# One core, one list of 865 steps: the order of a fused sequence-mixing kernel drawn up anew

## The chip, the cores and the metric

The kernel runs on one core of a Trainium2 chip. The metric is device time in microseconds of one execution; lower is better. TensorE (PE), VectorE (DVE), ScalarE (ACT), GpSimd (POOL) and the DMA queues of SyncE (SP) and ACT work side by side. Each engine takes its own instructions strictly in the order of the program and waits at an instruction until what that one needs is there.

## The reference

Two branches over the same input of 2048 rows and 512 columns, mixed by a gate per row. Branch `a` is a diagonal linear recurrence with complex states, branch `b` is linear attention with 32 heads of width 16 and softmax feature maps.

```
g = sigmoid((x * gate_w).sum(-1))
# a: Lam_bar = exp(exp(log_dt) * Lam);  Bu = x @ B_bar.T
#    h[t] = Lam_bar * h[t-1] + Bu[t];   a = 2 * (h @ Cmat.T).real + x * Dskip
# b: q, k, v = x @ wqkv;  pq = q @ w_phi;  pk = k @ w_phi    (per head)
#    phi = concat(softmax(p), softmax(-p));  kv = phi_k.T @ v;  z = phi_k.sum(rows)
#    b = (phi_q @ kv / (phi_q @ z + 1e-6)) @ wo
out = g * a + (1 - g) * b
```

## The kernel before

The rows are cut into 16 tiles of 128; tile `ti` holds rows of one residue modulo 8, so that the recurrence is carried eight rows at a time. The kernel is written as small generators, `st_k`, `st_g` and so on, each of which makes one tile's worth of a stage and stops (`yield`) after each piece. A string, `ORDER`, says in which order the pieces are taken: each entry names a generator (letters and number), and taking the entry runs it to its next stop. `@` gives the PSUM banks that the piece takes, `:D` moves the evacuation of PSUM from ACT to DVE, `:A` sends an output through ACT's DMA queue instead of SP's, and `F:n` puts n idle matmuls.

The engines PE, DVE, ACT and SP are under a manual schedule: the list is their program order. There is no other scheduler for them, so an entry that is moved in the list moves on each engine and queue that it uses.

The entries:

- `NI`, `NR`: loads of the imaginary and the real part of B, 512 KB each (L287). `l8` to `l15`: transposing loads of row tiles 8 to 15 of x (L232); tiles 0 to 7 are loaded ahead of the list. `R`: transposes of B (L291). `Q`: transposing loads of the q weights (L295). `C`: transposing loads of C (L299). `J`: copies of the loaded C into two arrangements X1 and X2, two copies of 256 KB each (L304); `J0` and `J1` need C0, C2, C4 and C6, `J2` and `J3` need C1, C3, C5 and C7. `O`: load of wo. All of these are issued by SP.
- `W`, `f`, `w`: weights transposed and folded with w_phi. `V`, `U`, `P` to `P4`, `i`, `M`, `D`: parameters of the recurrence; `P2`, `P3` and `i` take sines and cosines on ACT. `L` loads the activation table set with Exp and Ln again, behind the sines.
- `k`, `v`, `q`: projections of a tile and their evacuation. `x`, `n`: maximum, minimum and differences for the softmaxes on DVE; `e`, `E`: the exponentials on ACT; `s`, `S`: sums, Ln, Exp and the multiply. `x0` to `x4` and so on are the key groups; `xA`, `nA`, `eA`, `sA` and those with capital letters (`X1` to `S3`) are the four query groups of four tiles. Step 8 of `sA` and of `S1` to `S3` is the multiply of L567; steps 9 to 12 send the four tiles through transposes into `phT` (L579), by SP, but for the last two tiles of the run, which PE transposes (L574).
- `a`: sums over the rows of key features times values; `Y` takes them out as `KVm`.
- `g`: Bu of residue r and state block j, `z` the scan over the blocks of eight rows, `h` the states of each residue. `c`: scaling of X1 and X2 (two multiplies on ACT, L603, and a sum).
- `y`, `o`, `t`: the outputs of a tile. `y`: h times C (L734) and the skip term (L739). `o`: query features times KVm (L753), division by way of Ln and Exp, and the transposing of the result, by SP (L775) or for the last four tiles by PE (L770). `t`: the product with wo (L782), the scaling by the gate (L786 on ACT, L788 on DVE) and the output DMA (L790).

How an entry is read:

```
    for tok in ORDER.split():
        tok, _, eng = tok.partition(":")
        tok, _, banks = tok.partition("@")
        sel["eng"] = "dve" if eng == "D" else "act"
        sel["q"] = nc.scalar if eng == "A" else nc.sync
        ...
        next(st[tok])
```

Exponentials and logarithms go through `aexp`, sines through `asin`; both note for the program's builder that they come behind the table load that they belong to (L132).

Of the kernel before, what the change touches and what calls it, by code (L numbers as in the profile page):

```python
# [864 lines left out]
```

## Time and profile before

| | |
|---|---|
| time, median of 3 runs | 157.53 us |
| lowest, highest | 156.07, 159.17 us |
| span of the profiled execution, first to last instruction | 153.7 us |
| median less span | 3.8 us |
| PE busy | 145.5 us (95%) |
| DVE busy | 131.0 us (85%) |
| ACT busy | 136.7 us (89%) |
| POOL busy | 12.9 us (8%) |
| granted TensorE clock, mean | 0.995 |

The profile is of one execution; its own time outside the program is not shown, so its span stands for it, and the difference to the median, 3.8 us, is what lies around it. Sums below are made on the span. Busy time counts an instruction from its start to its end as recorded; instructions of one engine overlap at their ends, and the ends of matmuls are modelled, so an engine with 99% busy time may still have small gaps. A releaser is who ended an engine's wait.

### The profile page before, as it was taken

Reading aid. Unit: us, or ns where it says so; the run is one execution under the profiler, and the core shown is the slowest. Engines: PE = TensorE matmul, PEld = TensorE weight load, DVE = VectorE, ACT = ScalarE, POOL = GpSimd, SP = SyncE. Lnnn points to the kernel's source line nnn. Section 1 sums busy time; section 2 is a strip of 40 time slices with the busy share of each in tenths; the row PEclk is TensorE's granted clock in tenths of the full one; section 3 lists DMA queues with packets and bytes.
Section 4 is the critical chain, followed back from the end, with each engine's and each line's share of the span. In section 5 each row is a group of like instructions: output and inputs, shape, how many; then the busy total and the mean of one; then the engine's idle time right before and its main releaser. Section 6 shows DMA issues by size and latency. Waiting matters only on the chain.

```text
span 153.7 us, 3412 instructions
## 1 busy us (share of the span) xinstructions
PE 145.5 (95%) x1238; PEld 99.7 (65%) x1254; DVE 131.0 (85%) x302; ACT 136.7 (89%) x322; POOL 12.9 (8%) x43
## 2 busy tenths in 40 slices
PE   7799999999999999999999999999999899999990
PEld 7656665886899858889876565554545455555550
DVE  3599999999999999999999999999999858445510
ACT  3599999999999999999999999999798897577672
POOL 8258800000000000000000000000000000000000
PEclk9999999999999999999999999999999999999998
DMA  4788995544474379960000006603139938667633
GB/s 117 162 220 121 213 171 102 102 86 92 101 102 100 80 146 205 237 133 0 2 4 2 0 0 134 125 18 68 33 82 118 215 80 194 141 118 172 211 123 102
DMA packets 48737, 17.03 MB, mean 111 GB/s; under 512 B 42064, under 2 KB 48720, under 8 KB 48720
## 3 DMA queue, kind: packets, MB, share of 16 engines
q1 hardware_dynamic: 47008, 15.36, 50.6%
q10 hardware_dynamic: 1552, 1.44, 2.9%
q8 instruction: 10, 0.16, 0.5%
q0 software_dynamic: 160, 0.01, 0.2%
q14 instruction: 7, 0.06, 0.1%
HBM read 2.64 MB, written 2.10 MB: 31 GB/s over the span
## 4 chain that ended last, share of the span: by engine, by line
ACT 48%; PE 31%; DMA 8%; DVE 6%; issue 3%; POOL 2%; ACTq 0%; POOLq 0%
PE py L734 12%; ACT EEk L140 12%; ACT uv L121 9%; PE py L782 6%; ACT vx L121 5%; PE pq L478 5%; ACT Xq L121 5%; ACT phT L603 4%; PE ph L685 3%; ACT va L121 3%; DMA phT<-EEq 3%; DMA oT<-on 3%; PE pn L753 2%; DMA vec_n<-in_A_log_dt_dram 2%; ACT EEq L140 2%
## 5 line engine op out<-in xcount | busy, mean ns | idle before, releaser
L614 PE MATMUL pgq<-xT,BT 128*128 128x256 bf16 x256 | 31.5, 272 | 0.0
L614 PEld LDWEIGHTS <-BT 128*128 128x128 bf16 x256 | 24.7, 98 | 3.5
L140 ACT ACTIVATE EEk<-EEk 128x1024 bf16<-128x1024 bf16 x20 | 21.3, 1099 | 0.0
L478 PEld LDWEIGHTS <-xT 128*128 128x128 bf16 x128 | 12.2, 97 | 11.0 <-issue 0.2
L121 ACT CAST uv<-pgq 128x512 bf16<-128x512 f32 x28 | 16.7, 638 | 0.0
L492 PE MATMUL pv<-Wv,xT 128*128 128x256 bf16 (+1 forms) x128 | 16.5, 273 | 0.1
L478 PE MATMUL pq<-Wq,xT 128*128 128x512 bf16 x60 | 15.2, 379 | 0.2
L782 PE MATMUL py<-Wo,oT 128*128 128x512 bf16 x59 | 14.7, 379 | 0.6 <-DMA oT<-on 0.3
L478 PE MATMUL pk<-Wk,xT 128*128 128x512 bf16 x60 | 14.9, 379 | 0.2
L492 PEld LDWEIGHTS <-xT 128*128 128x128 bf16 x128 | 12.5, 98 | 3.1 <-issue 0.2
L786 ACT ACTIVATE ot<-py,G 128x512 bf16<-128x512 f32 x15 | 9.8, 684 | 2.9 <-PE py L782 2.4
L140 ACT ACTIVATE EEq<-EEq 128x1024 bf16<-128x1024 bf16 x12 | 11.8, 1084 | 0.3 <-DVE EEq L535 0.3
L603 ACT ACTIVATE phT<-X,dgB 128x512 bf16<-128x512 bf16 x16 | 11.1, 751 | 0.0
L140 ACT ACTIVATE ld<-pn 128x16 f32<-128x16 f32 x32 | 6.4, 204 | 5.2 <-PE pn L753 5.0
L121 ACT CAST vx<-pv 128x256 bf16<-128x256 f32 x32 | 10.7, 435 | 0.0
L121 ACT CAST nu<-pn 128x256 bf16<-128x256 f32 x26 | 10.0, 400 | 0.0
L556 DVE TENSOR_TENSOR EEk<-EEk,rck 128x4096 bf16<-128x4096 bf16 (+1 forms) x5 | 9.3, 1860 | 0.1
L121 ACT CAST Xq<-pq 128x512 bf16<-128x512 f32 x16 | 9.0, 604 | 0.4 <-PE pn L753 0.4
L782 PEld LDWEIGHTS <-oT 128*128 128x128 bf16 x64 | 5.7, 98 | 5.7 <-DMA oT<-on 0.5
L753 PEld LDWEIGHTS <-phT 128*128 128x128 bf16 x128 | 6.4, 97 | 4.6 <-DMA phT<-EEq 1.3
L761 DVE TENSOR_TENSOR on<-nu,rd 128x512 bf16<-128x512 bf16 x16 | 6.6, 422 | 2.6 <-ACT rd L140 2.1
L519 DVE TENSOR_TENSOR smk<-smk 128x512 bf16<-128x512 bf16 (+4 forms) x18 | 8.1, 449 | 0.1
(179 smaller groups left out, 322.9 us busy)
## 6 DMA issues: line engine op xcount, KB each, us to landing
X<-HM SPq DMA_DIRECT2D x8, 256.0 KB, 4.7
out_dram<-ot SPq DMA_DIRECT2D x9, 128.0 KB, 2.2
out_dram<-ot ACTq DMA_DIRECT2D x7, 128.0 KB, 2.0
C2r<-in_B_wqkv_dram ACTq DMA_DIRECT2D x2, 256.0 KB, 3.5
Wv<-in_B_wqkv_dram SPq DMA_DIRECT2D x1, 512.0 KB, 4.0
Bn<-in_A_B_im_dram SPq DMA_DIRECT2D x1, 512.0 KB, 5.5
Bn<-in_A_B_re_dram SPq DMA_DIRECT2D x1, 512.0 KB, 5.9
Wo<-in_B_wo_dram SPq DMA_DIRECT2D x1, 512.0 KB, 5.9
```

The source lines that it names most:

```text
L121: nc.scalar.copy(out=out_ap, in_=in_ap)
L140: ins = nc.scalar.activation(**kw)
L478: MM(out=pt[:], lhsT=xT[:, kt, ti * P:(ti + 1) * P], rhs=W[:, kt, :], start=(kt == 0), stop=(kt == KT - 1))
L492: MM(out=pv[c][:], lhsT=xT[:, kt, ti * P:(ti + 1) * P], rhs=Wvg[:, kt, c * hd:(c + 1) * hd + c], start=(kt == 0), stop=(kt == KT - 1))
L519: VT(out=dst, in0=cur[:, :, :, 0:n, :], in1=cur[:, :, :, n:2 * n, :], op=op)
L556: VT(out=E5, in0=E5, in1=rc.to_broadcast([P, L, 2 * NB, Dh, 4]), op=ALU.mult)
L603: nc.scalar.mul(out=t_, in_=x_, mul=c_)
L614: MM(out=pg[:, h, :], lhsT=BT[:, kt, 2 * j + h, :], rhs=xT[:, kt, r * NC:(r + 1) * NC], start=(h == 0 and kt == 0), stop=(r % 2 == 0 and k ...
L734: MM(out=py[:], lhsT=hs(r, t, slice(a * P, (a + 1) * P)), rhs=C2B[t], start=(t == 0), stop=False)
L753: MM(out=pn[:, 4 * m:4 * m + 4, :].rearrange("p h e -> p (h e)"), lhsT=ph[:, 4 * hf + m, :], rhs=KVm[:, 4 * hf + m, :], start=(m == 0), st ...
L782: MM(out=py[:], lhsT=oT[:, g, :], rhs=Wo[:, g, :], start=False, stop=(g == HG - 1))
L786: nc.scalar.mul(out=ot[:], in_=py[:], mul=G[:, ti:ti + 1])
```

## The change

The string `ORDER` is replaced. It holds the same 865 entries. Their order is another, many PSUM banks are, and 30 entries have another engine or output queue: the evacuations of W2 and f1 go from ACT to DVE, the other 28 belong to the tail (o7 to o15, S3, t3 to t15). In both lists every Exp and Ln that comes after the sines stands behind `L`. Nothing else in the kernel is changed. Lines that neither the text nor the prediction speaks of are left out here.

```diff
--- before.py
+++ after.py
@@ -22,34 +22,34 @@
 ORDER = """
-NI l8 l10 F:28 W1@0 W0@1 W0 B W2@2 W2 NR W1:D W3@3 f1@4 f1 W3:D V@5 V U f0@6 U P P P2 U P2 P2 P2 P2 f0 f2@0 P4 P4 P4
-V2@1 V2 f2 l9 P3 i3 f3@3 f3 F:4 k1@2 k0@4 P P2 P3 l12 i1 i0 k0 gw i0 i3 U k1 i3 i3:D i3 i0 i1 i1 k2@5 k2 k3@6 k3 v0@03
-k4@1 i0:D x0 i1:D l11 x0 i1 n0 F:4 x0 k4 n0 R0 i2 n0 i0 x0 n0 k5@4 i2 i2 x0 i2:D n0 x1 x1 k5 n1 i2 v3@25 v0 x1 k7@6 k7
-k6@7 R1 L e0 n1 n1 x1 n1 l13 k6:D v4@14 x1 l14 v1@03 v1 k10@6 n1 x2 v4 n2 n2 n2 x2 e0 s0 x2 v3 v7@70 v7 l15 k8@3 v2@14
-v6@25 s0 s0 k9@7 k12@0 x2 Q1 e1 s0 v2 v6 s0 k11@1 s0 e1 M k11 k8 D k10 k9 R3 k12 g40@4 g40 s0 s1 g00@2 g00 n2 a0@51 a0
-v5@36 v5 s1 R5 x2 v8@70 R2 v8 C5 s1 s1 s1 s1 g60@4 n2 x3 s1 g60 g30@2 x3 n3 x3 n3 g10@3 C3 g20@6 e2 e2 e2 e2 x3 a1 a1
...
-a2 s3 C6 g21 g62 C2 C1 g11 g11 C0 J0 w0@6 w1@0 J2 J2 a2 g22@4 J0 w2@2 x4 s3 J1 g31 w1 w0 w3@7 g22 g31 z0 z0 z0 s3 w2
-s3 n4 z0 z0 w3 g61@0 g51@6 g51 g61 g02@4 g51 e4 g02 g71@3 g71 g71 g71 q3@2 s3 g12@7 g12 e4 q2@0 z0 g12 z1 q3 q1@6 q1
-q0@4 q2 z1 z0 h50@3 z1 z1 g42@7 q0 z1 z1 v10@26 h50 xA z1 h10@0 e4 e4 z1 g42 nA s4 g32@4 v10 g32 a3 g52@3 g32 h60@7 c2
-xA s4 c4 O g52 xA c4 R6 z1 z1 v9@26 s4 h10 g52 nA g72@4 g72 c4 h60 v9 a3 J3 g03@3 v11@26 c2 c2 s4 g72 g72 c0 c0 nA
...
-g73 g73 v13@26 v13 q10@0 z3 c6 z3 c5 sA z3 z3 v15@73 z3 a4 a4 a4 v15 z3 q10 q5@4 a4 Y z3 h31@0 q5 sA h30@4 z3 q9@2 h31
-q13@6 h31 q9 h33@0 h61@7 Y q13 h30 sA sA c5 h62@3 z3 z3 h30 h61 sA Y Y h22@5 q4@2 h62 q4 h33 q15@6 q11@7 h22 h20@4 h20
-h32@2 h32 sA sA c1 q11 h13@1 h13 h32 q14@3 h40@5 h33 c3 h53@7 h42@4 sA h42 h53 c1 c1 sA h21@2 c3 h21 q6@0 q6 q15 c6
-q7@1 h63@4 h63 q8@7 h03@0 c3 q7 c6 h40 sA c7 h41@6 h41 y6@2 c7 h03 h03 h43@4 h43 y2@1 h02@5 c7 sA h23@6 h23 h01@0
...
-o3 G S1 N2 S1 t2 o3 S1 o3 t2 t2:A q12@3 q12 N2 S1 S1 o1@4 o1 o1 o1 o1 S1 S1 E2 S1 y0 y4@1 y9@3 y8@4 y8 y8 X3 E2 E2 S1
-S1 S1 N3 X3 E2 t3 X3 X3 X3 S2 N3 t0 t0 t0:A S2 t3 S2 y1 t1 t1 y5 y9 y9 o4@7 o4 o4@0 o4 y4 o4 o4 o4 o5@5 o5 o5@7 o5 o5
-y13@0 S2 S2 o6@5 o6 o6@7 o6 o6 y13 N3 y7@5 y7 N3 y7 y13 o5 S2 S2 N3 E3 o5 o6 o6 S2 S2 E3 E3 o7@7 o7:D y4 t4 t4:D t5
-o7@7 S2 S2 E3 S3 t5 S2 S3 S3 o7 o7 o7 t6 y11@1 y11 o7 t6 o8@6 o8 o8@7 o8 o8 S3 S3 o8 y12@2 o9@6 o9 o9@7 o8 y11 y12 y12
-y10@6 o9 o9 o9 o11@7 o11 o9 S3 S3 y10 y10 o11@7 t7 o11 o11 t7 t8 S3 S3 o11 o11 S3 t8 S3@7 S3:D S3@5 S3 t9 t9 t1:A
-o10@4 y15@7 o10:D o10@5 o10:D t8 o10 o10 o10 y15 o12@4 o12:D o12@3 t4 o14@5 o12 o12 o12 t5 o14 t11 o14@4 o14:D o14 o14
-t11 y14@3 t9:A o13@5 o13 o12@4 o12:D y14 o13@1 o13 o13 o15@4 o15:D o15@5 o15 o15 t12 t3:A t10 o13 o13@1 o15 t6:A t11
-o14@4 o13:D t7 t10 t10 y15 t12 t12 o15@5 o15 y14 o14:D t13 t14 t14 t14 t13 t13 t15 t15 t15:A
+NI B l8 NR F:28 W0@2 W0 W1@1 W1:D W3@5 W3:D W2@6 W2:D l10 f1@0 f1:D f3@4 V@1 V U f3 P P P2 f2@6 P2 P2 P2 f0@0 f0 P P2
+P4 P3 f2 P2 P4 V2@5 F:4 k1@3 k1 U l12 P4 V2 P3 i3 k0@4 i1 i0 gw l9 i0 k0 i3 i3 k2@1 k2 i1 i3:D i3 n0 i0 i0:D x0 n0 i1
+l11 x0 k3@6 R0 R1 n0 x0 k3 v0@03 v0 U n0 x0 R3 i1:D i2 k4@2 F:4 k4 x0 i0 i2 v1@75 n0 k5@4 i1 x1 n1 v1 k5 k6@3 i2 i2:D
+i2 L x1 k7@6 k7 l15 v3@25 e0 e0 v4@41 v4 R2 n1 x1 n1 x1 U k6:D v3 n1 x1 l13 n1 M k8@0 x2 Q1 n2 l14 x2 v7@63 v7 s0 C2
+e1 k10@7 k8 v2@41 n2 v6@25 s0 x2 s0 n2 s0 s0 v6 v2 D k12@6 s0 s0 e1 s1 g00@3 g40@2 n2 k10 k12 k11@0 k11 k9@4 s1 k9
...
+g70 g70 z0 C7 w0@6 w0 a2 a2 g62 s3 a2 z0 s3 g21 a2 g22@3 g22 g61@6 g31 J0 w1@0 z0 z0 z0 z0 C1 J1 x4 g41 g61 g31 z0 z0
+n4 w3@7 g51@3 w3 w1 s3 g51 g51 s3 g02@2 g02 w2@4 z0 w2 g71@6 g71 q1@7 s3 q0@4 z0 g12@0 C5 e4 g12 g71 g71 z1 e4 h10@3
+z1 g12 h50@6 q1 e4 h10 q3@2 q2@0 g42@7 z1 z1 h50 h60@3 z1 q0 z1 h60 q3 J3 a3 q2 xA nA z1 z1 g32@6 e4 g32 v10@02 J2 J2
+J0 g42 g32 c2 g52@3 g52 nA v10 v9@07 c2 g52 s4 xA nA c2 g72@4 s4 v9 xA c4 c4 z1 z1 s4 g72 c4 xA v12@03 v11@72 s4 g03@6
...
+g53 eA q5@0 g73@7 g73 g73 g73 sA z3 z3 v13@34 sA z3 z3 sA q10@6 v13 q10 v15@27 v15 a4 a4 a4 h22@4 q5 c3 c3 h22 a4 Y
+h62@7 h31@0 h62 sA q9@2 c0 z3 Y z3 c3 q9 h32@2 q4@3 q13@4 z3 z3 sA h31 h31 sA Y G h20@7 h32 h32 q4 q13 h20 Y c1 q8@5
+c1 q15@0 h42@4 h30@7 q7@6 q7 h42 q11@3 q15 O q11 h33@3 z3 z3 c1 h41@1 h30 q14@6 h41 h13@4 h13 h53@2 c6 sA h53 q6@0 h30
+h33 h21@1 c7 sA h33 c6 h21 h23@4 y2@7 q8 c7 h43@3 h23 c6 y6@2 h63@5 c7 sA sA q6 h40@1 sA h40 y6 y2 h02@4 q14 h02 y0@1
...
+t2 G o3@3 S1 o3 o3 t2 N2 S1 o3 S1 N2 S1 o0 t0 t0 N2 o1@4 o1 o1 S1 o3 q12@7 q12 S1 S1 y8@3 E2 y4@1 y4 o1 y9@4 t3 S1 o1
+S1 E2 E2 E2 y9 X3 t1 N3 y8 X3 N3 X3 N3 y4 S1 X3 t3 S1 t1 o4@7 o4 S1 N3 o4@0 y5 X3 S2 o4 o4 y8 y9 S2 o5@5 o5 o5@7 o5 o5
+y13@0 o4 o6@5 o6 o6@7 o6 S2 S2 o6 o5 y13 y13 S2 o4 o5 N3 y7@5 S2 S2 o6 o7@7 o7 y7 y7 o6 E3 E3 E3 o7@7 S2 t4 S2 E3 S2
+S2 o7:D t4:D t5 t5:D t6 t6:D y11@1 S2 y11 o8@7 o7 t6:A S3 o8:D o8@6 o7 o7 o8 y12@2 o8 S3 o9@7 o9 o8 o9@6 o9 o9 S3 y11
+S3 S3 S3 y12 y10@6 o9 S3 o11@7 y10 y10 o11 o11@7 o11 o8 o9 S3 o11 o11 t7 t7:D S3 o11 t2:A y12 t0:A S3 S3@7 S3 t8 t7
+S3@5 S3:D t5:A y15@7 t8 t9 t9:D o10@5 o10 o10@3 o10:D o10 y15 y15 o12@5 o10 o12:D o12@3 o12 t3 t11 t11:D o14@3 o12 o14
+o14@4 o14 o14 y14@5 o13@3 o15@4 o13 o12 o10 o13@1 o13 o15:D y14 o12@3 o15@4 o13 t1:A t10 o14 o13 o13@1 o12 o14@3 o15:D
+o15 o15 t10:D t12 o13 t13 o15@6 t9 t4:A t11:A o15:D o14 y14 t14 t12:D t12 t10:A t14 t13:D t13:A t14 t15 t15:D t15:A t8
 """
```

More of the change, by code (lines that the diff above doesn't have):

```diff
@@ L30 @@
-v5@36 v5 s1 R5 x2 v8@70 R2 v8 C5 s1 s1 s1 s1 g60@4 n2 x3 s1 g60 g30@2 x3 n3 x3 n3 g10@3 C3 g20@6 e2 e2 e2 e2 x3 a1 a1
-n3 Q2 k15@7 g10 g10 k15 x3 n3 g20 k14@0 k14 s2 n3 R4 s2 k13@4 g01@3 Q0 k13 n4 s2 g30 g01 x4 s2 x4 Q3 n4 x4 g50@7 g70@6
-g30 g50 n4 x4 e3 e3 g41@0 g50 n4 R7 s2 g21@4 s2 g70 s2 C7 e3 g31@3 e3 s3 g62@2 C4 g70 g70 z0 g11@7 a2 z0 s3 g41 z0 a2
-a2 s3 C6 g21 g62 C2 C1 g11 g11 C0 J0 w0@6 w1@0 J2 J2 a2 g22@4 J0 w2@2 x4 s3 J1 g31 w1 w0 w3@7 g22 g31 z0 z0 z0 s3 w2
-s3 n4 z0 z0 w3 g61@0 g51@6 g51 g61 g02@4 g51 e4 g02 g71@3 g71 g71 g71 q3@2 s3 g12@7 g12 e4 q2@0 z0 g12 z1 q3 q1@6 q1
@@ L35 @@
-q0@4 q2 z1 z0 h50@3 z1 z1 g42@7 q0 z1 z1 v10@26 h50 xA z1 h10@0 e4 e4 z1 g42 nA s4 g32@4 v10 g32 a3 g52@3 g32 h60@7 c2
-xA s4 c4 O g52 xA c4 R6 z1 z1 v9@26 s4 h10 g52 nA g72@4 g72 c4 h60 v9 a3 J3 g03@3 v11@26 c2 c2 s4 g72 g72 c0 c0 nA
-g63@0 z2 z2 v12@74 a3 nA v11 a3 xA g03 z2 z2 z2 z2 xA nA s4 J3 g63 g23@2 c5 s4 v12 g23 h51@6 g13@3 g13 g13 z2 z2 c0 z2
-z2 eA g43@0 g43 eA v14@74 v14 J1 h51 s4 g33@2 g33 h52@3 g33 h12@0 g53@6 eA g53 g53 h12 h11@7 h11 h52 eA sA g73@4 g73
-g73 g73 v13@26 v13 q10@0 z3 c6 z3 c5 sA z3 z3 v15@73 z3 a4 a4 a4 v15 z3 q10 q5@4 a4 Y z3 h31@0 q5 sA h30@4 z3 q9@2 h31
@@ L40 @@
-q13@6 h31 q9 h33@0 h61@7 Y q13 h30 sA sA c5 h62@3 z3 z3 h30 h61 sA Y Y h22@5 q4@2 h62 q4 h33 q15@6 q11@7 h22 h20@4 h20
-h32@2 h32 sA sA c1 q11 h13@1 h13 h32 q14@3 h40@5 h33 c3 h53@7 h42@4 sA h42 h53 c1 c1 sA h21@2 c3 h21 q6@0 q6 q15 c6
-q7@1 h63@4 h63 q8@7 h03@0 c3 q7 c6 h40 sA c7 h41@6 h41 y6@2 c7 h03 h03 h43@4 h43 y2@1 h02@5 c7 sA h23@6 h23 h01@0
-h00@4 END q8 G X1 y6 y6 q14 y2 N1 X1 h00 h00 N1 y2 h02 h02 X1 N1 G h01 o0@6 y0@7 o0 o0@3 h01 o2@4 o2 X1 o2@5 o2 o2 N1
-y5@6 o0 y3@0 X1 N1 y5 X2 o0 o1@4 E1 o2 y0 o2 o0 E1 E1 E1 X2 y1@5 y1 y3 y3 o1 G N2 X2 N2 X2 o0 N2 X2 o3@3 o3 o3@4 S1 o3
@@ new lines @@
+l11 x0 k3@6 R0 R1 n0 x0 k3 v0@03 v0 U n0 x0 R3 i1:D i2 k4@2 F:4 k4 x0 i0 i2 v1@75 n0 k5@4 i1 x1 n1 v1 k5 k6@3 i2 i2:D
+i2 L x1 k7@6 k7 l15 v3@25 e0 e0 v4@41 v4 R2 n1 x1 n1 x1 U k6:D v3 n1 x1 l13 n1 M k8@0 x2 Q1 n2 l14 x2 v7@63 v7 s0 C2
+e1 k10@7 k8 v2@41 n2 v6@25 s0 x2 s0 n2 s0 s0 v6 v2 D k12@6 s0 s0 e1 s1 g00@3 g40@2 n2 k10 k12 k11@0 k11 k9@4 s1 k9
+a0@51 g40 x2 a0 v5@67 v5 s1 x2 g00 R6 s1 Q3 R5 s1 n2 v8@04 v8 s1 x3 g20@2 s1 e2 e2 n3 e2 g10@7 k13@3 g10 x3 g10 n3 e2
+x3 n3 x3 C0 Q2 g01@6 g20 a1 a1 k15@0 k14@4 k15 R4 C4 g60@7 g30@2 Q0 n3 g01 x3 s2 g60 C3 g30 n3 s2 k13 k14 n4 g30 s2 n4
@@ new lines @@
+s2 x4 n4 x4 n4 e3 e3 C6 s2 s2 g11@6 x4 s2 g50@7 g50 g50 R7 e3 e3 g31@4 g11 g11 g70@3 s3 x4 g21@0 g70 g41@2 s3 g62@7
+g70 g70 z0 C7 w0@6 w0 a2 a2 g62 s3 a2 z0 s3 g21 a2 g22@3 g22 g61@6 g31 J0 w1@0 z0 z0 z0 z0 C1 J1 x4 g41 g61 g31 z0 z0
+n4 w3@7 g51@3 w3 w1 s3 g51 g51 s3 g02@2 g02 w2@4 z0 w2 g71@6 g71 q1@7 s3 q0@4 z0 g12@0 C5 e4 g12 g71 g71 z1 e4 h10@3
+z1 g12 h50@6 q1 e4 h10 q3@2 q2@0 g42@7 z1 z1 h50 h60@3 z1 q0 z1 h60 q3 J3 a3 q2 xA nA z1 z1 g32@6 e4 g32 v10@02 J2 J2
+J0 g42 g32 c2 g52@3 g52 nA v10 v9@07 c2 g52 s4 xA nA c2 g72@4 s4 v9 xA c4 c4 z1 z1 s4 g72 c4 xA v12@03 v11@72 s4 g03@6
@@ new lines @@
+g72 g72 z2 a3 a3 v11 s4 v12 z2 g03 c0 nA z2 h11@4 a3 g43@2 c5 z2 J1 c0 J3 g43 h11 xA nA g63@0 g63 g23@3 z2 z2 h51@6 s4
+g13@7 h51 z2 z2 g13 c5 c5 z2 v14@20 g33@4 g23 g13 g33 z2 v14 h61@7 eA g53@6 h61 h12@3 h12 g33 g53 h52@2 h52 s4 eA eA
+g53 eA q5@0 g73@7 g73 g73 g73 sA z3 z3 v13@34 sA z3 z3 sA q10@6 v13 q10 v15@27 v15 a4 a4 a4 h22@4 q5 c3 c3 h22 a4 Y
+h62@7 h31@0 h62 sA q9@2 c0 z3 Y z3 c3 q9 h32@2 q4@3 q13@4 z3 z3 sA h31 h31 sA Y G h20@7 h32 h32 q4 q13 h20 Y c1 q8@5
+c1 q15@0 h42@4 h30@7 q7@6 q7 h42 q11@3 q15 O q11 h33@3 z3 z3 c1 h41@1 h30 q14@6 h41 h13@4 h13 h53@2 c6 sA h53 q6@0 h30
@@ new lines @@
+h33 h21@1 c7 sA h33 c6 h21 h23@4 y2@7 q8 c7 h43@3 h23 c6 y6@2 h63@5 c7 sA sA q6 h40@1 sA h40 y6 y2 h02@4 q14 h02 y0@1
+h00@0 h00 h01@6 sA h02 h63 h03@5 h00 h43 END X1 o0@3 o0 N1 X1 h01 N1 h01 y0 y0 o0@0 o0 G X1 o2@4 o2 N1 h03 X1 y2 N1
+h03 X1 N1 X2 o2@6 o2 o2 o2 y6 y3@0 o0 G o2 E1 E1 E1 E1 X2 y3 y3 N2 y1@5 y1 y1 X2 y5@6 y5 o0 X2 N2 o1@3 o3@4 o1 o3 X2
+t2 G o3@3 S1 o3 o3 t2 N2 S1 o3 S1 N2 S1 o0 t0 t0 N2 o1@4 o1 o1 S1 o3 q12@7 q12 S1 S1 y8@3 E2 y4@1 y4 o1 y9@4 t3 S1 o1
+S1 E2 E2 E2 y9 X3 t1 N3 y8 X3 N3 X3 N3 y4 S1 X3 t3 S1 t1 o4@7 o4 S1 N3 o4@0 y5 X3 S2 o4 o4 y8 y9 S2 o5@5 o5 o5@7 o5 o5
```

## The prediction

> **What bounds the kernel now.** I read the page first, then busy time by stretches, then the waits, the chain that ended last and the order of the SP queue. Stretches: start:end, length, then busy us of PE, weight loads, DVE, ACT, POOL, granted clock, DMA share, GB/s.
>
> ```profile
> span 153.7 us, 3412 instructions
> 0.00:10.00 10.00, 7.81 (x73) 6.42 (x75) 5.66 (x37) 5.64 (x10) 4.92 (x17) 1.00 0.62 162
> 10.00:110.00 100.00, 99.13 (x849) 71.98 (x857) 98.95 (x216) 98.94 (x225) 8.01 (x27) 1.00 0.49 93
> 110.00:140.00 30.00, 29.09 (x233) 15.87 (x236) 21.81 (x40) 24.19 (x65) 0.00 (x0) 1.00 0.70 133
> 140.00:153.70 13.70, 9.52 (x88) 5.46 (x88) 4.57 (x12) 7.89 (x25) 0.00 (x0) 0.95 0.50 154
> ```
>
> From 10 to 110 us TensorE, VectorE and ScalarE are each busy for 99 of 100 us, at the full granted clock: no engine there has time to give away, and an order of the same work can win back only crumbs. From 110 to 140 PE is still busy 29.1 of 30 us while DVE and ACT have 8.2 and 5.8 us free. PE's idle time between 10 and 140 us is 0.87 + 0.91 = 1.8 us by these rows. The rest of its 8.2 us is the start (2.2) and the end (4.2).
>
> What times the stage after 110 us is seen in the chain, in the waits and in the SP queue.
>
> ```profile
> 112.31 2.84 ACT EEq L140 x3
> 115.15 4.63 DMA phT<-EEq
> ```
> ```profile
> PEld L753 <- DMA phT<-EEq: 1.3, 2, 0.9
> PEld L782 <- DMA oT<-on: 0.5, 1, 0.5
> ```
> ```profile
> 113.80 6.68 SPq L579 DMA_TRANSPOSE phT<-EEq  x4
> 121.02 4.25 SPq L775 DMA_TRANSPOSE oT<-on  x3
> 125.36 5.32 SPq L579 DMA_TRANSPOSE phT<-EEq  x4
> 130.78 4.58 SPq L775 DMA_TRANSPOSE oT<-on  x3
> ```
>
> From 113.8 to 135.4 SP issues fourteen transposes one behind the other. The two places where PE waits longest late in the run are landings of this series. Its first entry waits for step 8 of S1, which on DVE is this multiply:
>
> ```profile
> 112.41 1.22 DVE L567 TENSOR_TENSOR EEq<-EEq,rhoq 128x2048 bf16<-128x2048 bf16 x1
> ```
>
> It ends at 113.63 and SP starts at 113.80. So the end of the run is DVE's order up to S1's multiply, then SP's series, then a fixed tail. I compare the two lists along this line.
>
> **The change part by part.** The same 865 entries stand in both lists. 30 of them take another engine or another out queue: the W2 and f1 evacuations go from ACT to DVE, the rest lie behind 110 us. The act of the title itself costs nothing: in both lists all Exp and Ln entries after the sines stand behind L, the second load of the exponential set.
>
> ```profile
> 17.59 1.28 ACT L132 ACT_TABLE_LOAD   x1
> 18.89 1.06 ACT L140 ACTIVATE EEk<-EEk 128x1024 bf16<-128x1024 bf16 x1
> ```
>
> The load takes 1.28 us and the first exponential follows 0.02 us behind it. The number of loads stays three. The Trainium skill (ScalarE: Activation LUTs, What ACT_TABLE_LOAD costs) adds a drain of about 1.38 us to each switch. This trace shows none of it, and by either figure the sum is the same, since no load goes or comes.
>
> *Start.* DVE takes W2 and f1 over in a stretch where it is idle for 4.3 of 10 us. PE order and fold order stay (f1, f3, V, f2, f0 instead of f1, V, f0, f2, V2, f3).
>
> ```profile
> 5.97 0.42 DVE L123 COPY Xq<-ptw 128x512 bf16<-128x512 bf16 x1 [0.57 <-PE ptw L277]
> 6.98 0.17 DVE L315 CAST vec<-pvt 128x12 f32<-128x12 bf16 x1 [0.59 <-PE pvt L313]
> 18.20 0.68 DVE L123 CAST Xq<-pk 128x512 bf16<-128x512 f32 x1
> ```
>
> The three transposed W blocks now leave through DVE: by 0.4 us each from 5.3 on (an estimate), until 6.6. Then comes f1's cast from PSUM (0.68 us, as the third row, of the same shape): 6.6 to 7.2. The vec copy therefore starts near 7.2 instead of 6.98, and everything DVE does after it is a chain of small steps: **+0.2 us** (bounds 0, if the copies overlap as ACT's do, and +0.5). ACT loses two evacuations, by the chain's row for five in a row 0.48 us each:
>
> ```profile
> 26.98 2.42 ACT Xq L121 x5
> ```
>
> so ACT comes to L some 0.7 to 1.0 us earlier. It cannot keep this, as DVE feeds it (s, e) and is full. I count 0.
>
> *l10 is moved behind NR in the SP queue.* Rows: issue, duration, what; then the landing of single issues, in the order l8, l10, NR, l9.
>
> ```profile
> 13.15 2.83 SPq L232 DMA_TRANSPOSE xT<-in_A_x_dram  x2
> 16.03 0.61 SPq L287 DMA_DIRECT2D Bn<-in_A_B_re_dram  x1
> 16.68 3.92 SPq L232 DMA_TRANSPOSE xT<-in_A_x_dram  x3
> ```
> ```profile
> xT<-in_A_x_dram SPq DMA_TRANSPOSE x1, 5.2
> xT<-in_A_x_dram SPq DMA_TRANSPOSE x1, 4.2
> Bn<-in_A_B_re_dram SPq DMA_DIRECT2D x1, 512.0 KB, 5.9
> xT<-in_A_x_dram SPq DMA_TRANSPOSE x1, 5.7
> ```
>
> l8 lands at 13.15 + 5.2 = 18.35, l10 at 14.7 + 4.2 = 18.9, NR at 16.03 + 5.9 = 21.9, l9 at 16.68 + 5.7 = 22.4: each close behind the one issued before it. With NR in front, l10 lands about 3.0 us behind l8 plus 0.6: **21.9**. k10 needs it.
>
> ```profile
> 19.10 1.02 PE L478 MATMUL pk<-Wk,xT 128*128 128x512 bf16 x4
> ```
>
> k10 now runs at 19.1, just behind its landing. In the new list k8 (four such matmuls) and v7 (eight of half the width) stand ahead of it in addition. Eight of full width take
>
> ```profile
> 87.64 1.73 PE pq L478 x8
> ```
>
> so that is 1.73 us more, and PE comes to k10 at about 20.8: a wait of **1.1 us** (bounds 0, if l10 passes the block, as its 4.2 us alone would have it at 19.6, and 1.5). The Trainium skill (DMA: Bandwidth & Descriptors, Queues, rings and completion order) says that each DMA engine takes the descriptors of one ring in order. By that rule the wait is the 1.1 us; without it, none. The landings above agree with the rule.
>
> Behind k10 on PE are v2, v6, k12, g00. ACT wants v6 first: it has its 0.7 to 1.0 us of lead there, and loses it. DVE wants k10 only through x3, after k9, whose evacuation is one of the five in the last ACT row (26.98 to 29.40), so of the 1.1 us I put **+0.2** on the line (bounds 0 and 1.1).
>
> *The J copies come after C1, C5.* From the first BT transpose to the last C there are 22 issues now:
>
> ```profile
> 21.98 2.50 SPq L291 DMA_TRANSPOSE BT<-Bn  x2
> 50.63 1.26 SPq L299 DMA_TRANSPOSE HM<-in_A_C_re_dram  x1
> 53.16 5.18 SPq L304 DMA_DIRECT2D X<-HM  x5
> ```
> ```profile
> DMA to landing us min/median/max: 3.5/4.7/5.6
> ```
> ```profile
> 62.48 2.03 ACT L603 ACTIVATE phT<-X,dgB 128x512 bf16<-128x512 bf16 x3
> ```
>
> That is 29.9 us, 1.36 each. The new list has 21 of them, from 21.4, ahead of J0: 50.0. Then J0, C1, J1, C5 (0.7 + 1.3 + 0.7 + 1.3): 54.0. J3 has to wait for C5's landing, 2.5 us behind its start as J0 is behind the last C now: 55.3. Then J2, J2, J0 at 1.04 each (5.18 for five): the second J0 is issued at 58.4 and lands at **63.1** (61.9 to 64.0 by the row of landings). c2's second multiply needs it. Now c2 starts at 62.48 and all four copies lie landed. ACT's entries ahead of c2's second step in the new list, summed by their durations in this trace, are what ACT has behind it at 63.1 now. So the two meet: **+0.2** on the line (bounds 0 and 0.9); cover is gone, and each us more of landing is one of ACT's.
>
> *The middle otherwise.* Up to the first max of group 1 (X1), and up to the multiplies of S1 and S2, DVE has exactly the same entries ahead in both lists but W2 and f1, and ACT up to E1 the same without these two. Inside, entries trade places. The largest move: nine more entries, 3.4 us by their rows, go ahead of sA's multiply, so it starts at 93.6 instead of
>
> ```profile
> 90.23 1.22 DVE L567 TENSOR_TENSOR EEk<-EEk,rhok 128x2048 bf16<-128x2048 bf16 x1
> ```
> ```profile
> 91.47 7.43 SPq L579 DMA_TRANSPOSE phT<-EEk  x4
> ```
> ```profile
> phT<-EEk SPq DMA_TRANSPOSE x4, 3.1
> ```
>
> and its four transposes are issued from 94.9 to 98.7 and land, 3.1 us on, from 98.0 to 101.8. PE reads them in o0 to o3, of which o0 and o2 come first:
>
> ```profile
> 100.13 0.29 PE L753 MATMUL pn<-KVm,phT 128*128 128x68 bf16 x4
> 101.12 0.54 PE L753 MATMUL pn<-KVm,phT 128*128 128x68 bf16 x12
> ```
>
> In the new list o0 keeps its place, o2 moves to about 101.6 with its block landed at 100.5, o1 and o3 behind 108: hidden, with 1.1 us in hand for o2. The last issue is now held to 97.7 by c7 anyway. New crossings between the three engines can cost PE as much idle time again as it has, or give all of it back: **0**, bounds -1.8 and +1.8.
>
> *The tail.* o4 to o11, t4 to t15 stand on PE within 1.7 us of where they stood, and SP's series has the same order of transposes. Fourteen evacuations go to DVE (nine of them output scalings) and seven come back; DVE is free for 17 of the last 44 us. t6's out on ACT's queue comes in front of o8, when its scaling is done. The last:
>
> ```profile
> 148.80 1.84 ACT L786 ACTIVATE ot<-py,G 128x512 bf16<-128x512 f32 x3 [1.10 <-PE py L782]
> ```
>
> Now t13, t14 and t15 queue on ACT to 150.64. In the new list t13 and t15 are DVE's and t15's scaling starts as PE ends: **-0.2** (bounds -0.5 and +0.8, if the outs of t0 and t2, now issued near 135, delay the last transposes).
>
> *Sum* on the profiled execution: 153.7 + 0.2 + 0.2 + 0.2 + 0 - 0.2 = 154.1. The span is 3.8 under the median of the three runs, 157.53, so **157.9 us**. By the bounds: -2.3 and +5.1.
>
> **The rivals.**
>
> *The SP queue comes late and ACT stops at c2 (slower).* Its mechanism is the order of that one queue. If the J copies take 1.5 us each, the longest issue in the trace, and C5 0.6 more, the second J0 goes out at about 60.5 and lands, at 5.6, at 66.1. ACT then stands for 3.0 us at c2, with PSUM evacuations queued behind it, and PE and DVE stand too; with the 1.1 us at k10 in front it is 153.7 + 4.1, or **161.6**. It decides from a landing of about 63 on. For it: the copies lose all their cover of several us, and landings stretch when copies queue. Against: five issues in 5.18 us is what a crowded stretch shows.
>
> *The new order crosses better (a little faster).* If PE's 1.8 us of waits go and the SP items stay hidden: 153.7 - 1.8 = 151.9, so **155.7**. For it: on PE the distances between maker and user in 75 to 100 us (g53, y6, h00) are longer in the new list. Against: SP's series keeps its start, S1's multiply, unless DVE's own line gets shorter, and DVE has 1.05 us of idle in 100. More than 2% faster would need 3.2 us, nearly twice PE's idle time between 10 and 140.
>
> *It does nothing.* No exponential stood ahead of its load before, so only the reshuffle is left. If that is neutral too, 157.5, which a measurement could not tell from my forecast.
>
> **How the numbers follow.** No clear change, 157.9 with its own range 156.3 to 159.8: 0.62. Nothing at all, 157.5: 0.02. SP queue late, 161.6: 0.18. Better crossings, 155.7: 0.18. About 2%, or 3.15 us, is what a measurement of this kernel tells from no change. Below 154.4 I leave 0.04, from the tail of the better crossings; above 160.7 0.18: most of the SP rival and a little of the forecast. The range of 8 in 10 goes from 155.6 to 161.2.
>
> **What would show it.** Right: three table loads; PE waiting about 1 us at k10 near 21 us for xT; the second step of c2 starting close behind a landing of X; S1's multiply within 0.6 us of 112.4; PE, DVE and ACT again near 99 of 100 us from 10 to 110; the last scaling on DVE. Wrong: S1's multiply later than 114 (the middle lost time, in ACT's or DVE's idle rows), ACT idle by us at c2 (the SP rival), a fourth table load, or PE waiting for oT or phT for more than 2 us behind 115.

## The result, and the profile after

The change made the kernel slower: 162.22 us median (161.48 to 163.67, 5 runs) against 157.14 (156.07 to 159.17, 5 runs), a ratio of 1.0347 with a 95% interval of 1.0282 to 1.0411. The forecast was 157.9 with a range up to 161.2; the time lies above it. All ratios, and the medians of experiments 2 and 3, leave out single executions that took over 1.5% longer than the fastest of the same kernel (159.17 of before is one).

The profiled execution of before was a quick one. In every other execution whose span is on record the time is 1.95 to 2.13 us more than the span, so its 153.7 us answers to a time of about 155.8, below all five of before. Of the 3.8 us that the forecast put around the span some 2.0 lie there; the rest is that this execution was short. That of after is the slowest of its five (163.67; the spans of the five go from 159.5 to 161.6). So the two pages differ by 7.9 us where the medians differ by 5.1, and what is read off them below is somewhat too large. Stretches of the kernel after, columns as before (busy us of PE, weight loads, DVE, ACT, POOL, granted clock, DMA share, GB/s):

```profile
core 0 of [0], span 161.6 us
10.00:110.00 100.00, 96.26 (x833) 70.19 (x832) 95.30 (x211) 95.54 (x216) 9.20 (x26) 1.00 0.50 92
110.00:140.00 30.00, 27.38 (x208) 14.33 (x207) 24.37 (x47) 22.78 (x62) 0.00 (x0) 1.00 0.57 109
```

Where each engine was busy for 99 of 100 us it is now busy for 95 to 96. The clock is 1.00 as before; the engines wait for one another. The waits of after that are new or longer, from its view of waits (us in total, times, longest):

```profile
DVE nu L123 <- ACT ld L140: 4.3, 2, 3.2
...
PE py L734 <- DVE ot L788: 1.7, 1, 1.7
...
PE pn L753 <- DMA phT<-EEk: 1.3, 1, 1.3
...
PE pf L434 <- DMA HM<-in_B_wqkv_dram: 1.0, 1, 1.0
PE pk L478 <- DMA xT<-in_A_x_dram: 1.0, 1, 1.0
...
ACT phT L603 <- DMA X<-HM: 0.9, 1, 0.9
```

The first of them stood in the view of before too, with a larger total, but there no single wait was longer than 1.6 us:

```profile
DVE nu L123 <- ACT ld L140: 4.5, 3, 1.6
```

In order of time: k10 waits for l10 (22.55 us), w0 for the transpose Q0 (48.37), c2 on ACT for the X copies (66.70), o2 for sA's transposes (105.98), and DVE's nu copy of o7 for ACT (132.93), behind which PE's y11 waits for a bank. The same places in the timeline (start, duration, engine, what, and in brackets the idle time before it and what ended it):

```profile
22.55 1.04 PE L478 MATMUL pk<-Wk,xT 128*128 128x512 bf16 x4 [1.02 <-DMA xT<-in_A_x_dram]
...
48.37 0.40 PE L434 MATMUL pf<-BD,HM 128*128 128x128 bf16 x4 [1.04 <-DMA HM<-in_B_wqkv_dram]
...
66.70 0.72 ACT L603 ACTIVATE phT<-X,dgB 128x512 bf16<-128x512 bf16 x1 [0.89 <-DMA X<-HM]
...
96.99 1.22 DVE L567 TENSOR_TENSOR EEk<-EEk,rhok 128x2048 bf16<-128x2048 bf16 x1
...
98.23 5.45 SPq L579 DMA_TRANSPOSE phT<-EEk  x4
...
105.98 0.30 PE L753 MATMUL pn<-KVm,phT 128*128 128x68 bf16 x4 [1.33 <-DMA phT<-EEk]
...
117.71 1.23 DVE L567 TENSOR_TENSOR EEq<-EEq,rhoq 128x2048 bf16<-128x2048 bf16 x1
...
118.97 6.49 SPq L579 DMA_TRANSPOSE phT<-EEq  x4
...
128.53 1.23 DVE L567 TENSOR_TENSOR EEq<-EEq,rhoq 128x2048 bf16<-128x2048 bf16 x1
...
128.92 3.90 ACT L140 ACTIVATE EEq<-EEq 128x1024 bf16<-128x1024 bf16 x4
...
129.47 0.29 PE L753 MATMUL pn<-KVm,phT 128*128 128x68 bf16 x4
...
132.71 0.18 ACT L140 ACTIVATE ld<-pn 128x16 f32<-128x16 f32 x1
...
132.93 0.42 DVE L123 CAST nu<-pn 128x256 bf16<-128x256 f32 x1 [3.17 <-ACT ld L140]
133.27 2.06 DVE L788 TENSOR_SCALAR ot<-py,G 128x512 bf16<-128x512 f32 x3
...
135.24 1.22 DVE L519 TENSOR_TENSOR smq<-EEq 128x2048 bf16<-128x2048 bf16 x1
```

S1's multiply starts at 117.71 where it started at 112.41, and SP's series of transposes at 118.97 where it started at 113.80. So of the 7.9 us, 5.2 were lost ahead of the series and 2.7 behind its start. That splits the question in two, and the experiments took it up so.

### The profile page after: what moved, and what is told of

It is laid out like the page before. It is cut to its first block, busy times and chain, and to the rows that moved or that the text cites. A ratio compares the mean times of both kernels' runs of the same rounds, so it can differ in the third digit from the quotient of the medians.

```text
span 161.6 us, 3424 instructions
## 1 busy us (share of the span) xinstructions
PE 148.3 (92%) x1254; PEld 100.5 (62%) x1254; DVE 137.2 (85%) x311; ACT 132.6 (82%) x313; POOL 14.2 (9%) x43
## 4 chain that ended last, share of the span: by engine, by line
SPq 29%; ACT 26%; DMA 19%; PE 14%; DVE 5%; issue 3%; ACTq 1%; DVEq 0%
SPq L232 10%; SPq L291 6%; PE py L734 6%; SPq L299 6%; ACT phT L603 6%; PE py L782 4%; DMA Bn<-in_A_B_re_dram 4%; ACT EEq L140 4%; SPq L295 4%; DMA X<-HM 3%; DMA phT<-EEk 3%; DMA HM<-in_A_C_im_dram 3%; DMA phT<-EEq 3%; ACT Xq L121 3%; DMA oT<-on 3%
## 5 line engine op out<-in xcount | busy, mean ns | idle before, releaser
L614 PE MATMUL pgq<-xT,BT 128*128 128x256 bf16 x256 | 31.7, 272 | 0.0
L614 PEld LDWEIGHTS <-BT 128*128 128x128 bf16 x256 | 24.7, 98 | 3.9
L782 PE MATMUL py<-Wo,oT 128*128 128x512 bf16 x64 | 15.7, 379 | 1.4 <-DMA oT<-on 0.8
L478 PE MATMUL pk<-Wk,xT 128*128 128x512 bf16 x64 | 15.4, 379 | 1.0 <-DMA xT<-in_A_x_dram 1.0
L788 DVE TENSOR_SCALAR ot<-py,G 128x512 bf16<-128x512 f32 x10 | 7.2, 745 | 3.0 <-PE py L782 3.0
L753 PE MATMUL pn<-KVm,phT 128*128 128x68 bf16 x128 | 7.5, 194 | 1.9 <-DMA phT<-EEk 1.3
L121 ACT CAST Xq<-pk 128x512 bf16<-128x512 f32 x15 | 8.8, 609 | 0.4 <-PE pk L478 0.3
```

Of the source, the lines that this page charges most:

```text
L121: nc.scalar.copy(out=out_ap, in_=in_ap)
L478: MM(out=pt[:], lhsT=xT[:, kt, ti * P:(ti + 1) * P], rhs=W[:, kt, :], start=(kt == 0), stop=(kt == KT - 1))
L614: MM(out=pg[:, h, :], lhsT=BT[:, kt, 2 * j + h, :], rhs=xT[:, kt, r * NC:(r + 1) * NC], start=(h == 0 and kt == 0), stop=(r % 2 == 0 and k ...
L753: MM(out=pn[:, 4 * m:4 * m + 4, :].rearrange("p h e -> p (h e)"), lhsT=ph[:, 4 * hf + m, :], rhs=KVm[:, 4 * hf + m, :], start=(m == 0), st ...
L782: MM(out=py[:], lhsT=oT[:, g, :], rhs=Wo[:, g, :], start=False, stop=(g == HG - 1))
```

## The experiments

Ratios are to the kernel before on the same chip, with their 95% intervals; 1%, called a point below, is 1.57 us. Each edit moves entries of the list, or gives one or two of them another engine, and changes nothing else; a splice of two lists also renumbers a few PSUM banks. "S" is the theory that the SP queue's order costs the time, "T" that the late places do (sA's end and the tail), "C" that the new interleaving as such does.

**1. The SP queue in the old order, engines in the new one.** Shown are the entries of the SP queue alone, in their order.

```diff
-NI l8 NR l10 l12 l9 l11 R0 R1 R3 l15 R2 l13 Q1 l14 C2 R6 Q3 R5 C0 Q2 R4 C4 Q0 C3 C6 R7 C7 J0 C1 J1 C5 J3 J2 J2 J0 J1 J3 O
+NI l8 l10 NR l9 l12 l11 R0 R1 l13 l14 l15 Q1 R3 R5 R2 C5 C3 Q2 R4 Q0 Q3 R7 C7 C4 C6 C2 C1 C0 J0 J2 J2 J0 J1 O R6 J3 J3 J1
```

> The kernel after, with one thing undone: the first 42 entries of the SP queue (x loads, B loads and transposes, Q and C transposes, X copies, Wo) stand in the order of the kernel before; PE, DVE and ACT keep the new order. Theory S (the SP queue's order costs most of the 5.1 us): the waits for l10 (1.2 us of lag on PE), for Q0 at w0 (1.3) and for X at c2 (0.9 on ACT) go, and the median falls by 2.5 to 4, to about 158.5 to 159.5. Theory T (the tail costs most: the fourth step of o7 on DVE behind four exponentials, and sA's late transposes): the early waits go but the later ones take their place, and the median falls by less than 1.2, to 161 or more. Theory C (the new interleaving of the three engines itself has no slack, wherever it waits): no change within 0.5, 162.

163.64 us, 1.0436 (1.0378 to 1.0495): no gain, and not clearly a loss, as the intervals of this kernel and of after overlap. The waits of this kernel, against those of after:

```profile
DVE nu L123 <- ACT ld L140: 4.3, 2, 3.2
PEld L614 <- DMA BT<-Bn: 3.7, 3, 1.9
...
PE pgq L614 <- DMA BT<-Bn: 2.7, 3, 1.6
```

Q0 and X are no longer waited for, but the new PE order wants R0 to R3 (L614 reads BT) earlier than the old queue brings them, and DVE's wait in the tail stands as it was. S falls in the form it was put. T's "161 or more" holds; C's 162 within 0.5 was missed, but the run does not rule C out.

**2. The old engine order with the new SP order.** The reverse edit on the kernel before.

> The kernel before, with the SP queue's first 42 entries in the order of the kernel after; PE, DVE and ACT keep the old order. Theory S: the old order of the engines meets the same late landings, so it loses 2.5 to 4 us, to 159.5 to 161. Theory T: loses at most 1, 158. Theory C: also at most 1, since the loss belongs to the new interleaving; or, where the old engine order does not fit the new queue at all, more than 4.

159.16 us, 1.0186 (1.0119 to 1.0253). S's 159.5 to 161 was all but met, and the 158 that T and C allowed was passed. Together with the first run it says that each queue order fits its own engine order; neither order is slow by itself.

**3. o7's second nu copy back on ACT.** One entry.

```diff
-S2 S2 o7:D t4:D t5 t5:D
+S2 S2 o7 t4:D t5 t5:D
```

> The kernel after, with the fourth step of o7 (the second nu copy) on ACT as before, one entry changed. Theory T: the 3.2 us in which DVE stood for ACT's ld go, the three output scalings behind it start 3 us earlier, PE's wait at y11 (1.7 us) goes and the oT transpose of o7 is not held; the median falls by 1.5 to 2.5, to about 160. Theory S: the end is timed by S3's transposes, which come from S2 and S1, so what DVE wins it waits away; falls by at most 0.8, to 161.5. Theory C: 162.

159.21 us, 1.0191 (1.0142 to 1.0239): 1.6 points less than after, 2.4 us, from one entry. In its timeline the three scalings no longer stand behind ACT's exponentials:

```profile
127.20 1.23 DVE L567 TENSOR_TENSOR EEq<-EEq,rhoq 128x2048 bf16<-128x2048 bf16 x1
129.37 2.48 DVE L788 TENSOR_SCALAR ot<-py,G 128x512 bf16<-128x512 f32 x3 [0.94 <-PE py L782]
131.77 1.21 DVE L519 TENSOR_TENSOR smq<-EEq 128x2048 bf16<-128x2048 bf16 x1
```

They start 3.9 us sooner (129.37 against 133.27), and S3's first sum behind them 3.5 (131.77 against 135.24). Of both, 1.3 us are not the edit's: S2's multiply, which stands ahead of the edit, began at 127.20 against 128.53. The 2.6 and 2.1 us that are left fit the 2.4 us. T's number came.

**4. sA's end earlier.** rho behind Y, the multiply behind h42, the transposes behind q14, c6 and c7.

```diff
-... h20 Y c1 ... h42 q11@3 ... q14@6 h41 ... h53@2 c6 sA h53 ... c7 sA h33 ... h23 c6 y6@2 ... c7 sA sA q6 h40@1 sA h40 ... h01@6 sA h02
+... h20 Y sA c1 ... h42 sA q11@3 ... q14@6 sA sA h41 ... h53@2 c6 h53 ... c7 h33 ... h23 c6 sA y6@2 ... c7 sA q6 h40@1 h40 ... h01@6 h02
```

> The kernel after, with sA's rho, its multiply and its four transposes put ahead of the nine entries that the new list had set before them (rho behind the last entry of Y, the multiply behind h42, the transposes behind q14, c6 and c7). Theory S and T alike have the wait for phT at o2 (1.5 us of lag on PE) fall away; T: the median falls by 1 to 1.5, to 161; S: by 0.5 at most, because the entries that now come later (h13, h53, h41) are on PE's way in the same stretch; C: no change, 162, or slower.

159.95 us, 1.0249 (1.0198 to 1.0299): about 1 point, 1.5 us by the ratios, though this interval and that of after still touch. The multiply started at 91.03 and o0 and o2 ran with no wait:

```profile
91.03 1.22 DVE L567 TENSOR_TENSOR EEk<-EEk,rhok 128x2048 bf16<-128x2048 bf16 x1
...
100.69 0.29 PE L753 MATMUL pn<-KVm,phT 128*128 128x68 bf16 x4
...
102.13 0.42 PE L753 MATMUL pn<-KVm,phT 128*128 128x68 bf16 x8
```

T's number came again; S's "0.5 at most" did not.

**5. l10 alone ahead of NR.**

```diff
-NI l8 NR l10 l12 ...
+NI l8 l10 NR l12 ...
```

> The kernel after, with l10's issue ahead of NR's again, nothing else. If the wait at k10 (1.2 us of lag on PE) is carried to the end, the median falls by 1 to 1.2, to about 161; by the forecast's step (0.2 of the wait lies on the line) by 0.2, which is not seen; if NR, R0 and R1, now later, are wanted as early, it rises.

163.04 us, 1.0419 (1.0378 to 1.046): not faster, and of the three expectations the last came nearest. k10's wait shrank to 0.4 us on its weight load, and in its place g00 and g40 waited for R0 and R1, which wait for NR. Its waits from 17 to 30 us:

```profile
PEld L614 <- DMA BT<-Bn: 1.8, 2, 1.0
...
PE pgq L614 <- DMA BT<-Bn: 1.1, 2, 0.7
...
PEld L478 <- DMA xT<-in_A_x_dram: 0.4, 1, 0.4
```

**6. Three swaps in the SP queue.** l10 as in 5, Q0 and R6 exchanged, C1 and C5 ahead of the X copies.

```diff
-... C2 R6 Q3 R5 C0 Q2 R4 C4 Q0 C3 C6 R7 C7 J0 C1 J1 C5 J3 J2 J2 J0 J1 J3 O
+... C2 Q0 Q3 R5 C0 Q2 R4 C4 R6 C3 C6 R7 C7 C1 C5 J0 J2 J2 J0 J1 J3 J1 J3 O
```

> The kernel after, with three repairs of the SP queue's order that keep what the new engine order wants early: l10 ahead of NR, Q0 and R6 trade places, and C1 and C5 ahead of the X copies, which then go J0 J2 J2 J0 first. Theory S' (the three waits of 1.2, 1.3 and 0.9 us are real losses, and the old SP order only brought others in their place): the median falls by 1.5 to 3, to 159 to 160.5. Theory T (what is won before 70 us is waited away at sA's transposes and behind the four exponentials, which are placed on ACT's and DVE's own lines): falls by less than 0.8.

162.03 us, 1.0346 (1.031 to 1.0383), the same as after. T's half of the expectation held: what is won early is waited away at the places of 3 and 4.

**7 and 8. The repairs together.** 3 and 4; then 3, 4 and 6.

> The kernel after, with both the o7 step on ACT and sA's end earlier. If the two losses are separate, their gains add: 2.5 and 1.5 to 2 us, to about 157.8 to 158.5, 1% above before. If they are one loss seen twice (the same SP series behind both), the median stays near 159.5.

> The kernel after with the three swaps in the SP queue, the o7 step on ACT and sA's end earlier. If the five waits named from the trace are the whole loss, this is at before or a little under it, 155.5 to 157; if the new interleaving has a loss of its own beside them, 158 or more.

7: 158.61 us, 1.0126 (1.0089 to 1.0162). The two gains nearly add (1.6 and 1.0 points singly, 2.2 together). 8: 158.06 us, 1.0089 (1.0058 to 1.0121), at the edge of "158 or more": the five waits are not the whole loss. Q0 and X are waited for nowhere in it, but PE's waits at g00 and g40 are there:

```profile
25.56 0.61 PE L614 MATMUL pgq<-xT,BT 128*128 128x256 bf16 x4 [0.38 <-ACT vx L121]
26.86 1.48 PE L614 MATMUL pgq<-xT,BT 128*128 128x256 bf16 x12 [0.69 <-DMA BT<-Bn]
```

**11 and 12. On top of 8: g40 and g00 behind k9, then o14's evacuation ahead of two output issues on ACT.**

```diff
-g00@3 g40@2 n2 k10 k12 k11@0 k11 k9@4 s1 k9
+n2 k10 k12 k11@0 k11 k9@4 g00@3 g40@2 s1 k9
...
-t9 t4:A t11:A o15:D o14 y14
+t9 o14 t4:A t11:A o15:D y14
```

> The kernel with all three repairs (SP swaps, o7 step, sA's end), and in addition the first steps of g40 and g00 behind k9 on PE instead of ahead of k11. With l10 ahead of NR these two waited 1.5 us for the BT transposes, which wait for NR's landing. If that wait was the cost which the l10 swap brought in place of k10's, PE's lag at 27 us falls from 4.0 to about 2.5 and the median from 158.1 to 156.5 to 157; if k11 and k9 only wait in their place, no change.

> The previous kernel, and ACT's last oT evacuation (o14) ahead of the two output DMAs that ACT issued in front of it. The evacuation stood 1.5 us behind those issues, and PE's t14 0.6 us behind it. If the end hangs on it: another 0.4 to 0.6 us, to 156 to 156.5, level with before; if the last output's way out is what ends the run: no change.

157.5 us, 1.0059 (1.0038 to 1.008), and 157.41 us, 1.0045 (1.0021 to 1.007). The wait for BT is gone in both. The eleventh lies 0.5 us above the upper end of what was expected, and its interval overlaps that of 8. The twelfth missed its 156 to 156.5; its other branch, no change, came. From S1's series to the end, the twelfth kernel takes what before took: 114.26 to 154.2, 39.9 us, against 113.80 to 153.7.

```profile
114.26 6.53 SPq L579 DMA_TRANSPOSE phT<-EEq  x4
```

**9, 10, 13 to 16. Front of one list, tail of the other**, cut at END.

> All entries up to END in the order of the kernel after, all behind it in the order of the kernel before (four PSUM banks renumbered). Theory T (the new tail costs most of it, and the front's lag of some 2.8 us on PE is partly waited away by it): 158.5 to 160. If front and tail add up, this and the next one lie together 5.6 us above twice the time of before.

> All entries up to END in the order of the kernel before, all behind it in the order of the kernel after (one PSUM bank renumbered). sA's end and the SP queue are the old ones here, so only the o7 step behind the four exponentials and the rest of the new tail are left. Theory T: 2 to 3 us over before, 158.5 to 159.5. If the tail only hurts when the front is late: under 157.5.

> Old front, new tail (as two runs before), with the fourth step of o7 on ACT. If this one step is the loss of the new tail, 2.65% over before shrinks to 1% or less, 157 to 158 (0.6 us of it is a wait of y0 for q8 that the renumbered PSUM bank brings). If the rest of the new tail costs as much again, 159 or more.

> New front, old tail, with sA's rho, multiply and transposes earlier, and other PSUM banks than in the first splice, whose y2 waited 1.4 us for h21. Left in it are the waits for l10 and Q0 (1.2 and 1.3 us of lag) and X. If a lag on PE or ACT ahead of 70 us goes through to the end with the old tail too: 158 to 159, 1 to 1.5% over before. If the old tail's slack swallows it: under 157.5.

> The previous kernel with the three SP swaps and g40, g00 behind k9: the front repaired at all named places, the tail old. If the named waits are the whole loss of the front: level with before, 156.3 to 157.3, and 1.5 to 2 us under the previous kernel. If the new interleaving has a cost beside them: 158 or more.

> Old front, new tail with o7's step on ACT and o14's evacuation ahead of two output issues. If both new-tail waits named are all that it loses, it is level with before, 156.5 to 157.2; with the fifteenth scaling on DVE the end might even be 0.2 us sooner, as forecast. If o14 does not bear on the end: as the first kernel of these four.

| | kernel | us | ratio | interval |
|---|---|---|---|---|
| 9 | new front, old tail | 160.16 | 1.0241 | 1.0192 to 1.029 |
| 14 | and sA earlier, other banks | 158.88 | 1.0145 | 1.0103 to 1.0186 |
| 15 | and the queue and g repaired | 158.92 | 1.0139 | 1.008 to 1.0198 |
| 10 | old front, new tail | 160.63 | 1.0265 | 1.023 to 1.03 |
| 13 | and o7 on ACT | 159.23 | 1.0174 | 1.0128 to 1.0219 |
| 16 | and o14 earlier | 159.12 | 1.0161 | 1.0105 to 1.0217 |

By 9 and 10, front and tail each cost 2.4 to 2.7 points, 5.1 in sum, where the change costs 3.5. It could be that a late front hides part of a late tail, but the cut itself costs as well. 9 carried a wait of its own (y2 1.4 us for h21, through a renumbered bank), and 10 one of 0.6 us. 15 has the front of 11 and loses 1.4 points where 11 loses 0.6, and its waits from 90 to 112 us show new ones at the seam:

```profile
PE ph L685 <- DVE HM L689: 0.7, 1, 0.7
PE py L734 <- ACT Wk L121: 0.6, 1, 0.6
```

So these runs give bounds, not a clean division. Two things stand: o7's step is worth 0.9 points with the old front as well (10 against 13), and in 13, 15 and 16 the branch with a further cost came (159 or more, 158 or more, as 13), not the one within 1% of before or level with it. 14 came where a lag that goes through to the end was to put it; 9 and 10 came out above what T allowed them, 9 by 0.2 us and 10 by 1.1.

**17 and 18. Two terms of the forecast by themselves.** l10 behind NR in the kernel of 12; and in the kernel before the scalings of t13 and t15 on DVE.

> The best repaired kernel (twelfth run), with l10's issue put behind NR's as in the change. PE then waits at k10 for about 1.2 us. If an early wait on PE goes through to the end once the later waits are repaired: 158.2 to 158.6, 0.8 to 1.2 over the twelfth. By the forecast's step (0.2 of the wait lies on the line): 157.6.

> The kernel before with the output scalings of t13 and t15 on DVE (two entries), the one part of the change in which the forecast saw a gain. By the forecast: 0.2 us faster, bounds 0.5 faster and 0.8 slower. Rival: the last output's way out and SP's series set the end, and the scaling is not on it: no change within 0.15.

17: 157.31 us, 1.004 (1.0018 to 1.0063), no slower than 12, though PE stood 1.4 us at k10. So the 0.8 to 1.2 us of a wait that goes through did not come; a cost of 0.2 us would be too small to see. 18: 156.58 us, 0.9996 (0.9973 to 1.0019): no gain that can be seen; by the interval it is at most 0.27%, 0.42 us, so the 0.2 forecast can neither be shown nor ruled out.

No kernel here beats before; 18 is level with it, and the best repair of the new list, 17 or 12, is 0.4% above.

## Why the prediction was wrong

*The bound* was named rightly in its first two parts, S1's multiply and SP's series. The "fixed tail" was not fixed: from the start of the series to the end it is 42.6 us in after (118.97 to 161.6) and 39.9 in before. The forecast's own sign of failure came: S1's multiply later than 114 (117.71). What the prediction calls the act of the title, keeping the exponentials behind the load, cost nothing, as forecast: there are three loads, and the third takes 1.28 us as before.

```profile
18.11 1.28 ACT L132 ACT_TABLE_LOAD   x1
19.40 0.59 ACT L121 CAST Xq<-pk 128x512 bf16<-128x512 f32 x1
```

ACT goes on 0.01 us behind it, so the drain of about 1.38 us of which the Trainium skill speaks (ScalarE: Activation LUTs, What ACT_TABLE_LOAD costs) is not seen here either.

*"The tail: -0.2 us"* is the step that failed worst. It counted how much time DVE has free behind 110 us and not what a DVE copy waits for. In after, o7's second nu copy on DVE starts when ACT's ld, the other reader of the same PSUM bank, is done: DVE was free and PE had written pn by 129.76 (128.53 + 1.23, 129.47 + 0.29), ld ended at 132.89 and the copy began at 132.93. On the new ACT queue that ld stands behind the four exponentials of E3, and behind the copy on DVE stand three scalings and all of S3. Measured, in place of a gain of 0.2 us: 3.2 us of DVE, and 1.6 points (2.4 us) by the third run, 0.9 by the tenth against the thirteenth. The row to see it by was in the trace of before, at o7's other copy, which waited for one ld behind three exponentials:

```profile
126.14 0.42 DVE L123 CAST nu<-pn 128x256 bf16<-128x256 f32 x1 [1.61 <-ACT ld L140]
```

The next points use three pieces of the chain that ended last in the kernel after (start, duration, what):

```profile
15.33 6.70 DMA Bn<-in_A_B_re_dram
...
61.49 5.12 DMA X<-HM
...
100.97 4.97 DMA phT<-EEk
```

*"The middle otherwise: 0", sA's transposes "hidden, with 1.1 us in hand for o2"* failed next. The multiply was put at 93.6 and the third landing at 100.5; they came at 96.99 and 100.97 + 4.97 = 105.94, since DVE came to the multiply 3.4 us later than counted and the landing took 4.97 us where the working used 3.1. The fourth run prices it at 1 point. The bound of +1.8 us of that term would have held it; the value taken, 0, had no margin for any lag that came before.

*l10: +0.2* holds in size. The landing was forecast for 21.9 and the wait for 1.1 us; PE stood 1.02 us and began at 22.55. NR's load was done 15.33 + 6.70 = 22.03 us in, and k10 began 0.5 us behind that. The Trainium skill (DMA: Bandwidth & Descriptors, Queues, rings and completion order) has each DMA engine take the descriptors of one ring in order, and warns that completions need not come in that order; here they did. No cost of the wait can be seen in the seventeenth run, which could not tell 0.2 us from none, and taking the wait away alone only moved it to R0 (fifth).

*J: +0.2, landing at 63.1.* The second J0 copy went out at 61.49 and landed at 66.61, so the slower rival was right on the landing (66.1). Of the 3.5 us of delay 2.4 are one term of the working: it had J3 go 2.5 us behind C5's start, but SP stood for C5's landing until 4.9 us behind that start (54.42 to 59.28). The rival's price was not right: ACT stood for 0.89 us and not 3.0, as it came to c2 late itself (64.43 against 62.48). Its 161.6 lies near the time measured, but its mechanism is not the cause: with the queue's order undone (first run) or mended (sixth), the time stays. The wait of w0 for Q0, 1.04 us, was foreseen by no step. Mending these queue places, g40 and o14 is worth 0.8 points together, and only once the late places are mended (7 to 12).

*Start: +0.2* was not tried by itself. That ACT would come to L 0.7 to 1.0 us earlier did not happen: its load began at 18.11 where it began at 17.59.

In sum, of the 3.5 points: 2.2 are sA's end and o7's step (after to 7), 0.8 the queue with g40 and o14 (7 to 12), and 0.45 (0.21 to 0.70) remain, whose cause was not found. In the profiles of 17 and 18, one each, the series starts 0.6 us later in 17 (115.48 against 114.88), and the rest takes 0.3 us longer. The queue's share was not split up further: on the way from 7 to 8, 11 and 12 the interval of each overlaps that of the next.

## What to carry to other kernels

Before an evacuation goes to an engine with idle time, look on whose event it waits and what stands ahead of that event on the other engine's queue: here one 0.4 us copy cost 2.4 us by the third run. Where the engines are all busy, mend the latest wait first; a wait taken out early gave nothing as long as a later one stood. A queue order is only good with the engine order that it was drawn up for: swapping either one alone lost 1.9 points or gained nothing.
